# Batch 3's x transposed by VectorE from 128-byte pieces, and its whole x loaded eight steps later

## The chip, the cores and the metric

One core of a Trainium2 chip runs the kernel. The metric is device time in microseconds (us) of one execution; lower is better. TensorE's matmuls are called PE below, its weight loads PEld, VectorE DVE, ScalarE ACT, GpSimd POOL and SyncE SP; POOLq and SPq are the queues on which GpSimd and SyncE issue DMAs.

## The reference

Attention between x (4 batches, 8 heads, 512 tokens, 64 columns) and 32 state rows per head, read in both directions, then two MLPs one behind the other over all 2304 tokens (4 x 512 of x, 4 x 32 of state), each 512 to 2048 to 512:

```python
scores = scale * np.matmul(x, state.transpose(0, 1, 3, 2))
...
a /= a.sum(-1, keepdims=True) + 1e-09
xread = np.matmul(a, state)
scores2 = scale * np.matmul(state, x.transpose(0, 1, 3, 2))
...
sread = np.matmul(a2, x)
...
h = x @ w_in
g = h - np.tanh(h)
return (g @ w_out).astype(np.float32)
```

The second MLP has g = h * tanh(softplus(h)) in place of h - tanh(h). All inputs and outputs are float32.

## The kernel before

**The first MLP** runs as a list of steps (`seq`): batch 0 is steps 0 to 15, batch 1 steps 16 to 31, batch 2 steps 32 to 47, the state rows 48 to 51, batch 3 steps 52 to 67; layer 2 follows. A step makes one 128-row block of the hidden layer for 512 tokens: `up_x` multiplies into one PSUM bank h, in 6 matmuls of 128x512 (each float32 product is three: high by high, low by high, high by low, so that ath and atl are the attention's two halves and swh and swl the weights'); ScalarE takes tanh of the bank into t; VectorE subtracts (rows `t<-h,t` or, in another buffer, `wide<-h,wide`); ScalarE and VectorE split the difference into gh and gl. `down_x` of the step three before (`LA`) adds 12 matmuls into four banks acc. There are two banks h, so the matmuls of step i+2 overwrite what the subtraction of step i reads.

**Side work** is hung on a step by `at(step, f)` and issued behind its `up_x`, before the `down_x`. For batches 2 and 3 the list `when` (L1430) says at which step, counted from the start of the batch before, each of the twelve pieces of the attention comes: four turns of x (`XT[b, k]`, one per pair of heads k), the scores (`at_scores`, which calls `sc_m`, PE's matmuls into banks sct, and `sc_c`, the copies sct to scs), the softmaxes and the reads. Then `keep_pace` runs up to 3 (`MOST`) background pieces in a step, while at least 10 (`RESERVE`) slots are free: conversions of layer 2's weights (ACT `w<-st`, `r<-st`, `wh<-w`; DVE `w<-w,r`, `wl<-w,wh`, and half-size sums with tiles s), whose results POOL's queue stores to DRAM (`wi<-wh`, `wi<-wl`). Each engine works in the order in which it was issued.

**Turning x.** `at_xt` (batches 0, 1 and 3) makes four PE transposes of 128x128 into a PSUM bank xtp, rows `xtp<-ident,x`, and one ACT copy, `xt<-xtp`. They read the whole x, which `load_x` brings in four loads of 256 KB, on POOL's queue for batches 2 and 3 (L424, rows `x<-in_x_dram`, one of them into a buffer called wide). `xt_q` (batch 2 alone: `QUARTERS` is 2) is one DVE 32x32 block transpose of a 128x512 tile, `xt<-xq`, whose source `load_xq` has brought in eight DMAs of 32 KB on SP's queue (L447): each sets 32 partitions and reads 128 bytes at a time, laid out so that the block transpose alone gives the wanted order (its columns stand otherwise than those of `at_xt`, and `sc_c` sorts them out). The reading of state rows over x (`at_sread`) uses the whole x in either case.

**SP's queue** also carries the raw weights: `load_next` (L198) loads 512 KB into a stage st as soon as a conversion has read the stage's former contents, and DMAs behind it in the queue wait too.

**Pools.** 91 slots of 128x512 are handed out by `get`, oldest free first, or newest first where asked (`newest=True`), besides some half buffers.

Most engine instructions carry line 68, that of a helper which keeps their order. `load_x` is L416ff, `load_xq` L439 to L449, `xt_q` L451, `xt_t` and `xt_c` L457 and L466, `sc_m` L475, `sc_c` L493, `at_steps` L633, the loop that hangs them on steps L1431 to L1437, `keep_pace` L1444.

Of the kernel before, what the change touches and what calls it, by code (L numbers as in the profile page):

```python
# [31 lines left out]
QUARTERS = 2  # L32
# [48 lines left out]
def attention_moe_kernel(  # L81
# [16 lines left out]
    KD = DM // 128  # L98
# [24 lines left out]
    def get(name, dtype=F32, newest=False, whole=False):  # L123
        if halves and dtype == F32 and not whole:
            return halves.popleft()
        i = free.pop() if newest else free.popleft()
        return Unit(slots.tile([128, 512], dtype, tag=f"k{i}", name=name), i)
# [293 lines left out]
    def load_x(b, ks=range(KD)):  # L421
        for k in ks:
            u = get("x", newest=b > 1)
            (nc.gpsimd if b > 1 else nc.sync).dma_start(  # L424
                out=u.t.rearrange("p (h c) -> p h c", h=2),
                in_=x[b, 2 * k:2 * k + 2].rearrange("h (p r) d -> p h (r d)", r=4),
            )
            X[b, k] = u
# [10 lines left out]
    def load_xq(b, k):  # L439


        u = get("xq", whole=True)
        v = u.t.rearrange("p (i g d) -> p i g d", i=2, g=8)
        for i in range(2):
            src = x[b, 2 * k + i].rearrange("(l g e) (c d) -> (e c) l g d", g=8, e=2, c=2)
            for c in range(4):
                nc.sync.dma_start(out=v[c * 32:(c + 1) * 32, i], in_=src[c])  # L447
        P["q", b, k] = u
# [45 lines left out]
    def sc_c(b, i):  # L494
        SC[b, i] = get("scs")
        out = SC[b, i].t.rearrange("p (q e l h) -> p q e l h", q=2, e=2, h=4)
        for e in range(2):
            src = P["c", b][e][:, i * 256:(i + 1) * 256]
            if b == QUARTERS:
                src = src.rearrange("p (h q l) -> p q l h", h=4, q=2)  # L500
            else:
                src = src.rearrange("p (q l h) -> p q l h", q=2, h=4)
            evac(out[:, :, e], src, e if b else 1 - i)

    def at_scores(b):
        sc_m(b)
        for j in range(2):
            sc_c(b, j)
# [34 lines left out]
    def at_exp(b, j):  # L543
        sc_t(b, j)
        sc_max(b, j)
        sc_sub(b, j)
        sc_exp(b, j)
# [19 lines left out]
    def at_norm(b, j):  # L567
        nm_sum(b, j)
        nm_rec(b, j)
        nm_mul(b, j)  # L570

    def at_exp_t(b, j):
        e = SC.pop((b, j))
        mt = small.tile([128, 2], F32, tag="mt", name="mt")
        V.tensor_reduce(out=mt[:, 0:1], in_=e.t, axis=AX.X, op=ALU.max)
        V.tensor_scalar(
            out=mt[:, 0:1], in0=mt[:, 0:1], scalar1=-scale, scalar2=None, op0=ALU.mult
        )
        AC.activation(
            out=e.t, in_=e.t, func=ACTF.Exp, scale=scale, bias=mt[:, 0:1], accum_out=mt[:, 1:2]  # L580
        )
        V.tensor_scalar(
            out=mt[:, 1:2], in0=mt[:, 1:2], scalar1=1e-9, scalar2=None, op0=ALU.add
        )
        V.reciprocal(out=mt[:, 1:2], in_=mt[:, 1:2])
        V.tensor_scalar(
            out=e.t, in0=e.t, scalar1=mt[:, 1:2], scalar2=None, op0=ALU.mult
        )
        ET[b, j] = e

    def at_read_t(b, j):
        ps = side_bank("e2p")
        e = ET.pop((b, j))
        for r in range(4):
            TE.transpose(
                out=ps[:, r * 128:(r + 1) * 128],
                in_=e.t[:, r * 128:(r + 1) * 128],
                identity=ident,
            )
        u = get("e2")  # L600
        AC.activation(out=u.t, in_=ps, func=ACTF.Copy)
        put(e)
        ET[b, j] = u

    def at_sread(b):
        ps = side_bank("srd")
        u = [ET.pop((b, i)) for i in range(2)]
        for i in range(2):
            for r in range(4):
                for k in range(KD):  # L610
                    c = r * 128 + k * NS
                    TE.matmul(
                        out=ps[k * NS:(k + 1) * NS, i * 64:(i + 1) * 64],
                        lhsT=u[i].t[:, c:c + NS],
                        rhs=x_tile(b, k, i, r),
                        start=(r == 0),
                        stop=(r == 3),
                    )
        put(*u, *(X.pop((b, k)) for k in range(KD)))
        P["r", b] = o = get("sr")  # L620
        V.tensor_copy(out=o.t[:, :128], in_=ps[:, :128])

    def at_sturn(b):
        ps = side_bank("srt")
        u = P.pop(("r", b))
        TE.transpose(out=ps[:, :128], in_=u.t[:, :128], identity=ident)
        put(u)
        V.tensor_copy(
            out=xst[:, :, b * NS:(b + 1) * NS],
            in_=ps[:, :128].rearrange("p (k n) -> p k n", k=KD),  # L630
        )

    def at_steps(b):  # L633
        turn = xt_q if b == QUARTERS else at_xt
        return [lambda k=k: turn(b, k) for k in range(KD)] + [
            lambda: at_scores(b),
            lambda: (at_exp(b, 0), at_exp_t(b, 0)),
            lambda: at_norm(b, 0),
            lambda: (at_exp(b, 1), at_exp_t(b, 1), at_read_t(b, 0)),
            lambda: at_norm(b, 1),  # L640
            lambda: at_read_t(b, 1),
            lambda: at_sread(b),
            lambda: at_sturn(b),
        ]
# [115 lines left out]
    def evac(dst, src, i):  # L760
        if i % 2:
            return V.tensor_copy(out=dst, in_=src)
        return AC.activation(out=dst, in_=src, func=ACTF.Copy)
# [624 lines left out]
    def at(step, fn, back=None):  # L1388

        def held():  # L1390
            kept = [e.floor for e in engines]
            for e, m in zip(engines, marks[-back]):
                e.floor = m
            fn()
            for e, m in zip(engines, kept):
                e.floor = m

        side.setdefault(step, []).append(held if back else fn)

    seq = []  # L1400
    start = {}
# [18 lines left out]
    for j in range(2):  # L1420
        at(12 + j, lambda j=j: at_exp(1, j))
        at(13 + j, lambda j=j: at_norm(1, j))
        for b in range(2):
            k = start[1] + 4 + 2 * b + 4 * j
# [4 lines left out]
                at(k + 5, lambda b=b: at_sturn(b), 1)  # L1429
    when = {2: (3, 4, 5, 7, 8, 9, 10, 11, 12, 13, 15, 16), 3: (3, 3, 4, 5, 7, 8, 9, 11, 12, 12, 13, 15)}  # L1430
    for b in (2, 3):  # L1431
        if b == QUARTERS:
            for k in range(KD):
                at(start[b - 1] + when[b][k] - 3, lambda b=b, k=k: load_xq(b, k))
        at(start[b - 1] + (8 if b == QUARTERS else -1), lambda b=b: load_x(b))
        for i, f in zip(when[b], at_steps(b), strict=True):
            at(start[b - 1] + i, f)  # L1437
    for b in (1, 2, 3):
# [81 lines left out]
    def skip_banks(n):  # L1520
        ps_n[0] += n

    steps = {
        "x": lambda k: xt_t(0, k), "X": lambda k: xt_c(0, k), "s": lambda j: state_t(j, st[j]),
        "c": lambda j: sc_m(0), "C": lambda j: sc_c(0, j), "t": lambda j: sc_t(0, j),
        "m": lambda j: sc_max(0, j), "b": lambda j: sc_sub(0, j), "e": lambda j: sc_exp(0, j),
        "u": lambda j: nm_sum(0, j), "v": lambda j: nm_rec(0, j), "y": lambda j: nm_mul(0, j),
        "h": lambda j: at_a_hi(0, j), "l": lambda j: at_a_lo(0, j), "f": sw_first,
        "g": sw_first_lo, "z": skip_banks,
        "w": conv_first, "k": keep_warm, "p": lambda k: xt_t(1, k), "P": lambda k: xt_c(1, k),  # L1530
        "q": sc_m, "Q": lambda j: sc_c(1, j),
    }
    for e in (TE, AC, V):
# [153 lines left out]
```

## Time and profile before

| | |
|---|---|
| time, median of 3 runs | 702.04 us (700.21 to 702.95) |
| the profiled execution | 700.36 us, its span 698.6 us |
| granted TensorE clock | 0.999 |
| busy | PE 690.3 us (99%), DVE 514.9 (74%), ACT 366.0 (52%), POOL 90.6 (13%) |
| moved by DMA | 134.45 MB, mean 192 GB/s |

All times of the trace are us from the start of the span. Durations of single instructions overlap where an engine is pipelined: PE matmuls of 128x512 are recorded with 0.39 us each and start 0.23 us apart. "Idle before" is the time an engine stood still ahead of an instruction, with what ended it. The DMA share is the mean busy share of the 16 DMA engines; where a stretch is short it can come out a little over 1.

### The profile page before, as it was taken

To read this page: it belongs to the slowest core of one execution; us is meant where nothing else is said; L and a number is where in the kernel's file an instruction comes from. 1 tells how busy PE (TensorE), PEld (TensorE's weight loads), DVE (VectorE), ACT (ScalarE), POOL (GpSimd) and SP (SyncE) were. 2 spreads that over 40 slices of the span, in tenths; PEclk is the share of its full clock that TensorE was granted. 3 is DMA by queue.
4 is the path that set the end of the run, shared out by engine and by line. 5 is a ranking of instruction groups with operands and counts; after the bars stand their busy time and mean duration, and the time that the engine had idled before them with its cause. 6 is when DMAs were issued, how large, how long until landed. Compare 5 with 4: busy or idle time off the path is not lost.

```text
span 698.6 us, 11347 instructions
## 1 busy us (share of the span) xinstructions
PE 690.3 (99%) x4166; PEld 564.4 (81%) x4166; DVE 514.9 (74%) x904; ACT 366.0 (52%) x667; POOL 90.6 (13%) x136
## 2 busy tenths in 40 slices
PE   8999999999999999999999999999999999999998
PEld 6467777787777898778888888888888999999976
DVE  5899966796579847998476876767787555776784
ACT  6999644666576757877465432234424463433330
POOL 0000000116022323501222000111011000001000
PEclk9999999999999999999999999999999999999999
DMA  9886221318363677665959643667779676466303
GB/s 293 323 282 231 61 45 18 91 53 272 114 191 139 217 249 246 232 251 154 384 178 306 214 137 105 213 224 225 270 245 307 200 230 196 152 202 220 91 0 136
DMA packets 70952, 134.45 MB, mean 192 GB/s; under 512 B 16880, under 2 KB 27376, under 8 KB 70896
## 3 DMA queue, kind: packets, MB, share of 16 engines
q1 hardware_dynamic: 60656, 100.16, 44.2%
q0 software_dynamic: 10240, 33.56, 13.3%
q8 instruction: 33, 0.54, 0.3%
q14 instruction: 23, 0.19, 0.1%
HBM read 97.78 MB, written 35.91 MB: 191 GB/s over the span
## 4 chain that ended last, share of the span: by engine, by line
PE 42%; issue 37%; POOL 7%; ACT 5%; DVE 4%; DMA 4%; SPq 1%; POOLq 0%; ACTq 0%
PE acc L68 22%; PE h L68 15%; POOL wi L272 4%; POOL wo L272 2%; PE hs L68 2%; ACT r L68 2%; ACT w L68 2%; POOL wt L1149 1%; DMA x<-in_x_dram 1%; DMA wi<-wh 1%; DVE out L68 1%; DMA wide<-in_moe_w_out_dram 1%; PE swp L68 1%; DMA wt<-wl 1%; DVE wide L68 1%
## 5 line engine op out<-in xcount | busy, mean ns | idle before, releaser
L68 PE MATMUL h<-yh,ws 128*128 128x512 f32 x448 | 156.2, 392 | 0.1
L68 PE MATMUL acc<-wo,gh 128*128 128x512 f32 (+1 forms) x332 | 101.4, 387 | 0.4 <-DVE out L68 0.4
L68 PE MATMUL acc<-gh,wh 128*128 128x512 f32 x244 | 98.4, 403 | 0.0
L68 PEld LDWEIGHTS h<-yh,ws 128*128 128x128 f32 x448 | 84.3, 188 | 17.1 <-DVE wide L68 0.7
L68 PE MATMUL acc<-gh,wl 128*128 128x512 f32 x244 | 95.3, 391 | 0.0
L68 PE MATMUL acc<-gl,wh 128*128 128x512 f32 x244 | 95.2, 390 | 0.0
L68 PE MATMUL h<-yl,ws 128*128 128x512 f32 x224 | 87.6, 391 | 0.0
L68 DVE TENSOR_TENSOR gl<-wide,gh 128x512 fp32r<-128x512 f32 x79 | 53.6, 687 | 31.3 <-ACT gh L68 30.7
L68 PEld LDWEIGHTS acc<-wo,gh 128*128 128x128 f32 x332 | 61.9, 188 | 13.3 <-DVE out L68 0.8
L68 PE MATMUL acc<-wf,gh 128*128 128x256 f32 x384 | 70.5, 283 | 0.0
L68 ACT ACTIVATE wide<-wide 128x512 f32<-128x512 f32 x39 | 24.7, 633 | 83.0 <-DVE wide L68 83.0
L68 DVE TENSOR_TENSOR wide<-h,wide 128x512 f32<-128x512 f32 x76 | 52.1, 686 | 17.2 <-ACT wide L68 10.3
L68 PEld LDWEIGHTS acc<-wf,gh 128*128 128x128 f32 x384 | 62.0, 191 | 2.7
L68 PE MATMUL acc<-wo,gl 128*128 128x512 f32 (+1 forms) x166 | 64.2, 387 | 0.0
L68 PEld LDWEIGHTS acc<-gh,wh 128*128 128x128 f32 x244 | 45.8, 188 | 18.2 <-issue 4.2
L68 ACT ACTIVATE wide<-h 128x512 f32<-128x512 f32 x41 | 24.3, 593 | 61.9 <-PE h L68 55.1
L68 PE MATMUL acc<-wf,gl 128*128 128x256 f32 x192 | 54.3, 283 | 0.0
L68 PEld LDWEIGHTS acc<-gh,wl 128*128 128x128 f32 x244 | 45.8, 188 | 10.0
L68 PEld LDWEIGHTS acc<-gl,wh 128*128 128x128 f32 x244 | 45.9, 188 | 9.0 <-issue 0.4
L68 PE MATMUL h<-ath,swh 128*128 128x512 f32 x128 | 51.5, 403 | 1.2 <-ACT swh L68 1.2
L68 ACT ACTIVATE gh<-wide 128x512 fp32r<-128x512 f32 x79 | 48.4, 629 | 7.6 <-DVE wide L68 6.4
L68 PE MATMUL h<-ath,swl 128*128 128x512 f32 x128 | 50.5, 395 | 0.5 <-DVE swl L68 0.5
(220 smaller groups left out, 1289.3 us busy)
## 6 DMA issues: line engine op xcount, KB each, us to landing
ws<-wi SPq DMA_DIRECT2D x128, 256.0 KB, 4.5
st<-in_moe_w_in_dram SPq DMA_DIRECT2D x26, 512.0 KB, 5.4
wo<-wo SPq DMA_DIRECT2D x48, 256.0 KB, 4.1
st<-in_moe_w_out_dram SPq DMA_DIRECT2D x23, 512.0 KB, 5.0
wi<-wh POOLq DMA_DIRECT2D x32, 256.0 KB, 3.9
wi<-wl POOLq DMA_DIRECT2D x32, 256.0 KB, 4.4
wf<-wt SPq DMA_DIRECT2D x24, 256.0 KB, 5.1
wf<-wo SPq DMA_DIRECT2D x24, 256.0 KB, 3.7
```

Source lines behind the costliest of these rows:

```text
L68: i = fn(*args, **kw)
L272: nc.gpsimd.dma_start(out=d, in_=v if len(d.shape) == 2 else v.rearrange("p (g e) -> p g e", g=2))
L1149: nc.gpsimd.dma_start(out=D2T[g][:, 2 * j:2 * j + 2, h, :], in_=u.t.bitcast(F32).rearrange("p (i e) -> p i e", i=2),)
```

## The change

Batch 3's turn of x is done as batch 2's is. All four `load_xq(3, k)`, 32 DMAs of 32 KB, are issued at step 31; `xt_q` takes the place of `at_xt` at the same steps (35, 35, 36 and 37); the four whole loads of x move from step 31 to step 39, where the first user left is `at_sread` at step 45. `sc_c` sorts the columns for both batches.

```diff
@@ -439,7 +439,7 @@
     def load_xq(b, k):
 
 
-        u = get("xq", whole=True)
+        u = get("xq", newest=b > QUARTERS, whole=True)
         v = u.t.rearrange("p (i g d) -> p i g d", i=2, g=8)
         for i in range(2):
             src = x[b, 2 * k + i].rearrange("(l g e) (c d) -> (e c) l g d", g=8, e=2, c=2)
@@ -496,7 +496,7 @@
         out = SC[b, i].t.rearrange("p (q e l h) -> p q e l h", q=2, e=2, h=4)
         for e in range(2):
             src = P["c", b][e][:, i * 256:(i + 1) * 256]
-            if b == QUARTERS:
+            if b >= QUARTERS:
                 src = src.rearrange("p (h q l) -> p q l h", h=4, q=2)
             else:
                 src = src.rearrange("p (q l h) -> p q l h", q=2, h=4)
@@ -631,7 +631,7 @@
         )
 
     def at_steps(b):
-        turn = xt_q if b == QUARTERS else at_xt
+        turn = xt_q if b >= QUARTERS else at_xt
         return [lambda k=k: turn(b, k) for k in range(KD)] + [
             lambda: at_scores(b),
             lambda: (at_exp(b, 0), at_exp_t(b, 0)),
@@ -1429,10 +1429,12 @@
                 at(k + 5, lambda b=b: at_sturn(b), 1)
     when = {2: (3, 4, 5, 7, 8, 9, 10, 11, 12, 13, 15, 16), 3: (3, 3, 4, 5, 7, 8, 9, 11, 12, 12, 13, 15)}
     for b in (2, 3):
-        if b == QUARTERS:
-            for k in range(KD):
-                at(start[b - 1] + when[b][k] - 3, lambda b=b, k=k: load_xq(b, k))
-        at(start[b - 1] + (8 if b == QUARTERS else -1), lambda b=b: load_x(b))
+        for k in range(KD):
+            at(
+                start[b - 1] + (when[b][k] - 3 if b == QUARTERS else -1),
+                lambda b=b, k=k: load_xq(b, k),
+            )
+        at(start[b - 1] + (8 if b == QUARTERS else 7), lambda b=b: load_x(b))
         for i, f in zip(when[b], at_steps(b), strict=True):
             at(start[b - 1] + i, f)
     for b in (1, 2, 3):
```

How the instructions stand. **PE** around the first two turns, step 35, before (acc is numbered by bank):

```order
659 L68 MATMUL h<-atl,swh 128x512
660 L68 MATMUL h<-ath,swl 128x512
661 L68 MATMUL xtp<-ident,wide 128x128 x4
662 L68 MATMUL xtp<-ident,x 128x128 x4
663 L68 MATMUL acc_2215<-gh,wh 128x512
664 L68 MATMUL acc_2215<-gl,wh 128x512
```

and with the change:

```order
659 L68 MATMUL h<-atl,swh 128x512
660 L68 MATMUL h<-ath,swl 128x512
661 L68 MATMUL acc_2231<-gh,wh 128x512
662 L68 MATMUL acc_2231<-gl,wh 128x512
663 L68 MATMUL acc_2231<-gh,wl 128x512
```

The sixteen transposes of steps 35 to 37 are gone (3651 PE instructions before, 3635 now), and nothing else in PE's order moves.

**SP's queue** from the last pieces of batch 2's x on, the difference:

```order
 L447 DMA xq<-in_x_dram 32x8x32 x32
 L198 DMA st<-in_moe_w_in_dram 128x1024
-L198 DMA st<-in_moe_w_out_dram 128x1024 x4
+L198 DMA st<-in_moe_w_out_dram 128x1024 x3
+L447 DMA xq<-in_x_dram 32x8x32 x20
+L198 DMA st<-in_moe_w_out_dram 128x1024
+L447 DMA xq<-in_x_dram 32x8x32 x12
 L198 DMA st<-in_moe_w_in_dram 128x1024 x4
```

Twenty of the new DMAs (tiles 0, 1 and half of tile 2) stand before a load of raw weights into a stage, twelve behind it.

**DVE** from the second of the four new transposes on (steps 34 to 38; each `t<-h,t` is the subtraction of a step), with the change:

```order
251 L68 STREAM_TRANSPOSE xt<-xq 128x512
252 L68 SCALAR_TENSOR_TENSOR w<-w,r 128x512 x2
253 L68 TENSOR_TENSOR t<-h,t 128x512
254 L68 TENSOR_TENSOR wl<-w,wh 128x512
255 L68 TENSOR_TENSOR gl<-t,gh 128x512
256 L68 SCALAR_TENSOR_TENSOR w<-w,r 128x512
257 L68 TENSOR_TENSOR wl<-w,wh 128x512 x2
258 L68 TENSOR_TENSOR t<-h,t 128x512
259 L68 STREAM_TRANSPOSE xt<-xq 128x512
260 L68 TENSOR_TENSOR gl<-t,gh 128x512
...
264 L68 TENSOR_TENSOR gl<-t,gh 128x512
265 L68 STREAM_TRANSPOSE xt<-xq 128x512
```

and before, over the same steps:

```order
250 L68 SCALAR_TENSOR_TENSOR w<-w,r 128x512
251 L68 TENSOR_TENSOR t<-h,t 128x512
252 L68 TENSOR_TENSOR gl<-t,gh 128x512
253 L68 TENSOR_TENSOR t<-h,t 128x512
254 L68 TENSOR_TENSOR gl<-t,gh 128x512
255 L68 TENSOR_TENSOR wl<-w,wh 128x512
256 L68 SCALAR_TENSOR_TENSOR w<-w,r 128x512
257 L68 TENSOR_TENSOR t<-h,t 128x512
258 L68 TENSOR_TENSOR wl<-w,wh 128x512
259 L68 TENSOR_TENSOR gl<-t,gh 128x512
```

The first new transpose stands behind the subtraction of step 33, the second behind the copies y that end batch 1, the third behind the subtraction of step 36, the fourth behind the split of step 37. Conversions of layer 2's weights come earlier: from the copies y to the first transpose `a<-scs` (of the scores, around step 39) VectorE has six rows `w<-w,r` where it had four, five `wl` where it had three, four half-size sums where it had none, and the three later transposes. ScalarE loses its four copies `xt<-xtp`.

## Rows read from the trace of the kernel before

**Rows 1.** The page: busy time, and busy share and granted clock in 40 slices.

```profile
PE 690.3 (99%) x4166; PEld 564.4 (81%) x4166; DVE 514.9 (74%) x904; ACT 366.0 (52%) x667; POOL 90.6 (13%) x136
...
PE   8999999999999999999999999999999999999998
...
PEclk9999999999999999999999999999999999999999
```

**Rows 2.** Stretches, steps 35, 36, 37 and 41: us, busy by engine, clock, DMA share, GB/s.

```profile
181.57:186.57 5.00, 5.00 (x28) 4.21 (x26) 3.05 (x5) 3.55 (x7) 0.54 (x1) 1.00 0.32 105
186.57:191.14 4.57, 4.57 (x23) 3.77 (x22) 1.65 (x3) 1.75 (x4) 0.04 (x1) 1.00 0.17 61
191.14:195.68 4.54, 4.54 (x23) 3.77 (x22) 3.10 (x5) 3.31 (x6) 1.44 (x3) 1.00 0.54 160
210.43:214.51 4.08, 4.08 (x20) 3.38 (x19) 4.08 (x10) 2.38 (x5) 1.58 (x2) 1.00 0.82 312
```

**Rows 3.** Timeline of PE, steps 35 and 36: start us, us, engine, operation, count.

```profile
182.93 0.60 PE L68 MATMUL xtp<-ident,wide 128*128 128x128 f32 x4
...
184.03 0.40 PE L68 MATMUL acc<-gl,wh 128*128 128x512 f32 x1
...
187.93 0.60 PE L68 MATMUL xtp<-ident,x 128*128 128x128 f32 x4
...
188.60 0.40 PE L68 MATMUL acc<-gl,wh 128*128 128x512 f32 x1
```

**Rows 4.** The tile xtp: ns min/median/max of one, first and last start.

```profile
L68 ACT ACTIVATE xt<-xtp x10: 589/596/608, 6.6 to 193.2; 128x512 f32<-128x512 f32 x10
```

**Rows 5.** The tile xq, batch 2's pieces and their transposes.

```profile
L447 SPq DMA_DIRECT2D xq<-in_x_dram x32: 561/607/803, 87.3 to 108.3; - x32
...
L68 DVE STREAM_TRANSPOSE xt<-xq x2: 702/704/706, 106.1 to 115.5; 128x512 f32<-128x512 f32 x2
...
DMA to landing us min/median/max: 2.1/2.4/2.9
```

**Rows 6.** Stretches: a step of batch 1, the load's stretch, steps 35 to 43.

```profile
104.66:108.73 4.07, 4.07 (x19) 3.37 (x19) 4.00 (x11) 1.94 (x4) 0.00 (x0) 1.00 0.35 54
165.00:170.00 5.00, 5.00 (x34) 4.06 (x23) 3.74 (x9) 3.07 (x6) 4.70 (x8) 1.00 0.93 319
170.00:175.00 5.00, 5.00 (x24) 4.13 (x23) 4.05 (x8) 2.36 (x5) 3.09 (x5) 1.00 1.02 355
182.54:206.27 23.73, 23.73 (x151) 18.16 (x150) 13.18 (x23) 15.22 (x29) 3.28 (x6) 1.00 0.40 133
205.00:225.00 20.00, 20.00 (x102) 15.63 (x101) 19.97 (x46) 13.96 (x28) 4.65 (x7) 1.00 0.55 184
```

**Rows 7.** Timeline of SyncE's queue, 182 to 193 us.

```profile
182.53 0.33 SPq L198 DMA_DIRECT2D st<-in_moe_w_out_dram  x1
192.35 0.33 SPq L198 DMA_DIRECT2D st<-in_moe_w_in_dram  x1
```

**Rows 8.** Timeline of ScalarE, 181 to 184 us.

```profile
181.84 0.67 ACT L68 ACTIVATE w<-st 128x512 f32<-128x512 f32 x1
```

**Rows 9.** Timeline of the POOL queue, 160 to 205 us.

```profile
165.44 2.16 POOL L424 DMA_DIRECT2D x<-in_x_dram  x3 [0.30 <-PE srd L68]
```

**Rows 10.** DMA issues by kind: queue, count, KB each, median us to landing.

```profile
x<-in_x_dram POOLq DMA_DIRECT2D x7, 256.0 KB, 3.4
...
wide<-in_x_dram POOLq DMA_DIRECT2D x1, 256.0 KB, 6.6
```

**Rows 11.** Timeline of VectorE: start us, us, operation, idle before and its releaser.

```profile
178.47 0.69 DVE L68 TENSOR_TENSOR wide<-h,wide 128x512 f32<-128x512 f32 x1 [2.05 <-ACT wide L68]
...
188.76 0.69 DVE L68 TENSOR_TENSOR t<-h,t 128x512 f32<-128x512 f32 x1 [2.82 <-ACT t L68]
...
194.95 0.68 DVE L68 TENSOR_TENSOR gl<-t,gh 128x512 fp32r<-128x512 f32 x1
...
209.97 0.68 DVE L68 TENSOR_TENSOR t<-h,t 128x512 f32<-128x512 f32 x1
```

## The prediction

> **What bounds the kernel now.** First the page: PE is busy 690.3 us of 698.6 and in every slice but the first and the last at nine tenths or more, at the full granted clock [rows 1]; DVE is busy 74%, ACT 52%. So the program lasts as long as PE's list of work, unless another engine makes PE wait. The stretches of steps 35 to 37 say the same of the place of the change: PE is busy through all of 5.00, 4.57 and 4.54 us, at clock 1.00, while DVE works 3.05, 1.65 and 3.10 of them and ACT 3.55, 1.75 and 3.31 [rows 2]. A plain step, such as the 41st, is 4.08 us for its 18 matmuls [rows 2], 0.227 each. What is taken from PE's list there should come off the end; what is put on DVE or DMA costs only if PE then waits.
>
> Over its own span the profiled execution has 1.8 us (700.36 against 698.6), and it lies 1.7 us under the median of 702.04. I work out differences in the trace and set them against the median.
>
> **PE's transposes go (16 matmuls).** Step 35 has two groups of four: from the first group's start to the second matmul of acc, 182.93 to 184.03, is 1.10 us [rows 3]; one matmul of that is there anyway (0.23), so the two groups cost 0.87. Steps 36 and 37 have one each: 187.93 to 188.60 is 0.67, less 0.23 is 0.44 [rows 3], and twice 0.44 is 0.88. Sum 1.75. By whole steps: 5.00 + 4.57 + 4.54 less three times 4.08 is 1.87 [rows 2]. I take 1.8; the ends are 1.75 and 1.87. All of it is on the path, since PE works throughout. PE's order is otherwise as before.
>
> The Trainium skill, "VectorE: DVE Perf Modes", section "Rules for kernel authors", speaks against the change: a 128x128 transpose belongs on TensorE if PSUM will do as its destination, and the DVE is for 32x32 blocks. The rows agree on the durations, 0.44 us of PE a tile against 0.70 of DVE [rows 3, 5]; they differ from the rule in which engine has time left. The case in which the rule would hold here is part of the first rival.
>
> **DVE's four transposes come.** Each is 0.70 us [rows 5], 2.8 in all, and with them ACT's four copies of 0.60 go [rows 4]. The difference in order also brings weight conversions forward: between 182.54 and 206.27 DVE gets two more `w`, two more `wl`, four half sums and three of the transposes. At about 0.69 for a full row [rows 11], and 0.4 for a half one (an estimate: a fixed share and half the columns), that is 4 x 0.69 + 4 x 0.4 + 3 x 0.70 = 6.5 us. DVE is busy 13.18 of these 23.73 us [rows 6]; 10.5 are free, so it fits. I cost it at nothing. The cover is the two banks h: the subtraction of step 36 ends at 188.76 + 0.69 = 189.45 [rows 11] and its bank is written again at 195.68, the end of step 37 [rows 2], 6.2 us later. The precedent: batch 2's transposes ran between 106.1 and 115.5 on DVE [rows 5], and a step there is 4.07 us long with DVE busy 4.00 of it [rows 6]. If the cover were gone, each transpose would cost PE 0.70.
>
> **The pieces on SP's queue.** 32 DMAs at 0.61 us [rows 5] are 19.5 us of queue. Their slots come free when the reads `srd` of step 31 have ended; the whole loads of x waited for the same thing and went out at 165.44 [rows 9]. The first 20 then go out from 165.5 to about 177.7. Tile 0 is complete 8 x 0.61 later plus a landing of 2.4 to 2.9 [rows 5], at about 173; even with the 6.6 us of the load of x that landed slowest [rows 10] it is 177. DVE meets it behind the subtraction of step 33, about 175, and if it waited to 177 it would still be in front of the next subtraction at 178.47, ahead of which it stood idle 2.05 us [rows 11]. Tile 1, out by 175.2, is wanted only at step 34's end, about 182.5.
>
> Then comes the new wait. A raw load stands in front of the last twelve pieces, and it waits for the ACT conversion `w<-st` that ends at 181.84 + 0.67 = 182.51 [rows 8]; it went out at 182.53 [rows 7]. Behind it the twelve go out from 182.86 to 190.2. Tile 2 lands by 182.86 + 4 x 0.61 + 2.9 = 188.2, tile 3 by 193.1. DVE reaches the third transpose behind the subtraction of step 36 (189.45, or about 188.5 with PE 0.9 us earlier) and the fourth behind the split of step 37 (194.95 + 0.68 = 195.6 [rows 11], or 194.2 with PE 1.4 earlier). Margins of 0.3 and 1.1 us, and behind them the bank's 6 us. So I cost this at nothing; the ends are nothing and, if each landing took 6.6 us in place of 2.9 [rows 10], 3.7 less 0.3 of DVE's time, which the 6.2 still cover. The raw load behind the last pieces went out at 192.35 before [rows 7], since its stage was not free earlier; the pieces are out by 190.2.
>
> **DMA traffic.** Before, the whole loads fell into a stretch that was full (shares 0.93 and 1.02 [rows 6]). Now the first 20 pieces, 0.64 MB, fall there. Batch 2's moved 54 GB/s at a share of 0.35 [rows 6], 154 GB/s for a full share, against 319 at 0.93, or 343. So they take 0.64/154, 4.2 us of all engines, where 1 MB at 343 took 3.1: about 1 us more traffic. POOL's stores can be later by as much; PE reads none of what they carry before layer 2. The whole loads go to step 39, about 200, and land by some 207 [rows 10]; `at_sread` is at step 45, over 20 us on. Nothing for both.
>
> The Trainium skill, "DMA: Bandwidth & Descriptors", section "Specifications", holds that transfers below 512 bytes fall short of line rate. The rows of batch 2 agree, 154 against 343 GB/s for a full share; by the rule and by the rows alike the price is DMA time, which PE pays only if a tile is late.
>
> **Sum.** -1.8 + 0 + 0 + 0: 702.04 - 1.8 = 700.2 us (profiled 700.36 - 1.8 = 698.6).
>
> **The rivals.**
>
> *DVE gives it back.* Between 205 and 225 DVE is busy 19.97 of 20 us [rows 6]. The subtraction of step 40 ends at 209.97 + 0.68 = 210.65 [rows 11], its bank is written again at 214.51 [rows 2]: 3.9 us of slack, and 2.1 once PE is 1.8 us ahead and DVE is not. If the earlier conversions go on inside this stretch, three more (each a `w` and a `wl`, 1.4 us) are 4.2 us, and PE waits 2.1: 702.3; with five 7.0, a wait of 4.9 and 705.1. Were DVE without time from the turns on, four transposes of 0.70 less the 1.8 would be a loss of 1.0, 703.0. (That is the case of the Trainium skill's rule on transposes, named above.) For it: the full stretch. Against: conversions done early are not done again later, and 10.5 us are free ahead of it. Chance 0.15, times 701.5 to 705.
>
> *Slower, by SP's queue.* The raw load holds twelve pieces back for as long as its stage is not read. If that conversion is put off, tile 3 comes later by as much, DVE stops in front of it in order, and once 1.1 us and the bank's 6.2 are used up PE waits: from 7.3 us on it costs, from 9.1 on it has eaten the gain. Three steps of delay, 12.2 us, give 702.04 - 1.8 + 4.9 = 705.1; four give 709. For it: the queue waits in order, and conversions come in bursts when slots come free. Against: the difference in order brings conversions forward, not back, and ACT has less to do. Chance 0.07.
>
> *No effect.* PE's transposes might hide in a wait that PE would have anyway: 702.0. Against it, the matmuls behind them follow at once [rows 3]. Chance 0.06.
>
> *More than removed.* With the copies off ACT and the loads spread, some wait elsewhere might shrink: 3.6 us or more, 698.4 or less. But PE shows hardly a wait to shrink, only 8.3 us in the span, at its ends [rows 1]. Chance 0.06.
>
> **How the numbers follow.** The forecast keeps 0.66. A measurement tells changes over 0.5%, 3.5 us, from none, so the forecast, no effect and most of the first rival (up to 705.5) are "same": 0.65 + 0.06 + 0.13, and 0.02 of the second rival. Faster is the last rival, 0.06, and 0.01 of the forecast's spread: 0.07. Slower is the second rival but for its mildest cases, 0.05, and the first one's tail, 0.02: 0.07. Same is the rest, 0.86. The range: below, 700.2 less the 1.87 end and the 1.7 us by which executions lie under their median, 698.0. Above, it takes in no effect and the nearer part of the first rival, 703.2; left out are about 0.19: the last rival's 0.06, and 0.13 of the first two.
>
> **What would show it.** Right: no `xtp` in steps 35 to 37, which come down to about 4.1 us each, PE's matmuls fewer by 16, and DVE transposes of 0.70 that wait for a DMA less than 2 us. Wrong, by the first rival: PE idle "until DVE t" in 205 to 225. By the second: the fourth transpose starts after 200 and PE waits at step 39. If steps 35 to 37 shorten and the time does not fall by 1.4 us or more, a later stretch has taken it, and the first sum is wrong in its claim that nothing behind PE is short.

## The result and the profile after

| | before | with the change |
|---|---|---|
| time, median of 6 runs each | 701.4 us (700.21 to 702.95) | 710.57 us (707.22 to 712.93) |
| ratio to before | | 1.0125, 95% interval 1.0102 to 1.0148 |
| the profiled execution, its span | 700.36 us, 698.6 us | 711.1 us, 709.3 us |

The kernel is 9.2 us slower, where 1.2 us faster than this median was forecast (700.2), and outside the range. The page, the rows that answer to [rows 1]:

```profile
PE 693.4 (98%) x4150; PEld 565.9 (80%) x4150; DVE 517.9 (73%) x908; ACT 363.4 (51%) x663; POOL 90.8 (13%) x136
...
PE   8999999999997999899999999999999999999998
...
PEclk9999999999998999999999999999999999999999
```

PE's share has fallen, though its list of work is shorter: two slices (from 213 and from 284 us) are below nine tenths, and the granted clock has an eight among its nines. The waits of PE from 180 us to the end, first with the change and then before (us in all, times, longest):

```profile
PE e2p L68 <- DVE swl L68: 4.3, 1, 4.3
PE h L68 <- DVE t L68: 2.7, 1, 2.7
PE acc L68 <- DVE y L68: 0.7, 1, 0.7
```

```profile
PE acc L68 <- DVE out L68: 0.4, 1, 0.4
```

Before, PE waited once there, 0.4 us; that wait is there with the change too. Beside it PE now stands three times, before banks that DVE should have read. Where the time went is read from the starts of the same `up_x` matmuls in both traces (us from the span's start):

```
step    before   change   difference   since the row above
35      181.57   182.10   +0.53
38      195.68   194.34   -1.34        -1.87   the transposes
43      219.85   218.51   -1.34         0.00
44      224.42   229.99   +5.57        +6.91   wait before e2p, half clock
52      269.13   275.70   +6.57        +1.00   wait before acc
55      282.63   293.69   +11.06       +4.49   wait before h, half clock
end     698.6    709.3    +10.7        -0.4
```

The +0.53 is there from 34 us on, before any row that the change touches, and is of the execution. The stretches that answer to [rows 2] (steps 35 to 37) and [rows 6], and the two around the first wait (busy us of PE, PEld, DVE, ACT and POOL, then clock, DMA share, GB/s):

```profile
182.10:186.19 4.09, 4.09 (x20) 3.38 (x19) 4.04 (x7) 3.87 (x8) 0.57 (x1) 1.00 0.53 156
186.19:190.26 4.07, 4.07 (x19) 3.38 (x18) 3.81 (x6) 2.92 (x6) 2.70 (x5) 1.00 0.80 243
190.26:194.34 4.08, 4.08 (x19) 3.38 (x18) 3.17 (x5) 2.99 (x6) 0.84 (x2) 1.00 0.94 272
205.00:225.00 20.00, 15.74 (x80) 11.79 (x79) 15.59 (x33) 11.36 (x23) 6.57 (x10) 0.94 0.68 238
219.67:224.33 4.66, 0.41 (x3) 0.01 (x1) 4.55 (x9) 2.80 (x6) 1.45 (x2) 0.83 0.38 135
224.33:230.00 5.67, 5.67 (x17) 4.62 (x18) 5.67 (x14) 4.62 (x9) 0.86 (x1) 0.54 0.09 30
```

The three steps are 4.09, 4.07 and 4.08 us, as forecast. From 205 to 225, where DVE was full before, it works only 15.59 of 20 us and PE 15.74. From 219.67 PE does next to nothing for 4.66 us, and in the 5.67 us behind it the granted clock is 0.54.

**The chain behind the first wait**, from PE back. PE, the matmul in front of the wait and the one that ends it:

```profile
219.67 0.40 PE L68 MATMUL h<-ath,swl 128*128 128x512 f32 x1
224.33 0.90 PE L68 MATMUL e2p<-ident,scs 128*128 128x128 f32 x3 [4.25 <-DVE swl L68]
```

The bank of e2p (the transposes of a softmax's scores) had held the products swp of step 42, and DVE had not yet split them. DVE, the subtraction of step 41 and that split (a row's idle time stands in brackets with what ended it):

```profile
217.64 0.69 DVE L68 TENSOR_TENSOR t<-h,t 128x512 f32<-128x512 f32 x1 [1.93 <-ACT t L68]
...
223.59 0.68 DVE L68 TENSOR_TENSOR swl<-swp,swh 128x512 fp32r<-128x512 f32 x1
```

DVE waited for ScalarE's tanh, 217.02, though the h of step 41 was complete at 210.6. From there it worked without a gap to the split (4.55 of the 4.66 us in which PE stood), late by what it had waited. ScalarE, in the order in which it was issued:

```profile
206.56 0.66 ACT L68 ACTIVATE w<-st 128x512 f32<-128x512 f32 x1 [2.29 <-DMA wi<-wh]
...
210.10 0.68 ACT L68 ACTIVATE r<-st 128x512 uint32<-128x512 uint32 x1 [0.78 <-DMA wi<-wl]
...
211.39 0.58 ACT L68 ACTIVATE t<-h 128x512 f32<-128x512 f32 x1
...
216.46 0.66 ACT L68 ACTIVATE r<-st 128x512 uint32<-128x512 uint32 x1 [2.90 <-DMA wi<-wl]
217.02 0.59 ACT L68 ACTIVATE t<-h 128x512 f32<-128x512 f32 x1
```

Three conversions of layer 2's weights, `w<-st` and `r<-st`, stood 2.29, 0.78 and 2.90 us until stores of other weights, wi, had landed. They write into slots that those stores still read. The tanh of steps 40 and 41 (211.39 and 217.02) stand behind them. The chain of waits names the first of these stores:

```profile
201.38 5.10 DMA wi<-wh
...
206.56 0.13 ACT w L68
```

It was issued at 201.38 and took 5.10 us. Before, in the same steps, the tanh of step 40 began at 209.04 and the one wait of ScalarE for a store was 0.88:

```profile
209.04 0.58 ACT L68 ACTIVATE t<-h 128x512 f32<-128x512 f32 x1
...
212.20 0.63 ACT L68 ACTIVATE wh<-w 128x512 fp32r<-128x512 f32 x1 [0.88 <-DMA wo<-wh]
```

The wait of PE at 284 us is of the same kind: a split of layer 1's output, `yh<-wide`, waits 5.05 us for a store, and the tanh of step 52 behind it is 8 us behind its matmuls:

```profile
284.80 0.63 ACT L68 ACTIVATE yh<-wide 128x512 fp32r<-128x512 f32 x1 [5.05 <-DMA wo<-wl]
285.34 0.58 ACT L68 ACTIVATE t<-h 128x512 f32<-128x512 f32 x1
```

In the compiled order, each wait can be followed to the store that it names. In steps 39 to 42, three instructions of ScalarE and VectorE wait for stores of the last two steps before the change, and nine with it. What the forecast called harmless on DVE, conversions that come earlier, is the difference: by step 42 the change has done 29 background pieces, the kernel before 24 (20 against 15 by step 36).

The tile xq, to [rows 5]:

```profile
L68 DVE STREAM_TRANSPOSE xt<-xq x6: 702/704/712, 106.6 to 195.6; 128x512 f32<-128x512 f32 x6
...
  DMA xq<-in_x_dram: 1.1, 1
...
DMA to landing us min/median/max: 2.1/2.6/7.2
```

The pieces land up to 7.2 us after issue, and the last tile kept DVE 1.08 us; no wait of PE comes of it.

### The profile page after: what moved, and what is told of

Same layout as the page of the kernel before. It is cut to its first block, busy times and chain, and to the rows that moved or that the text cites. A ratio compares the mean times of both kernels' runs of the same rounds, so it can differ in the third digit from the quotient of the medians.

```text
span 709.3 us, 11372 instructions
## 1 busy us (share of the span) xinstructions
PE 693.4 (98%) x4150; PEld 565.9 (80%) x4150; DVE 517.9 (73%) x908; ACT 363.4 (51%) x663; POOL 90.8 (13%) x136
## 4 chain that ended last, share of the span: by engine, by line
PE 70%; issue 12%; ACT 6%; POOL 5%; DVE 4%; DMA 3%; SPq 0%; POOLq 0%; ACTq 0%; DVEq 0%
PE acc L68 38%; PE h L68 28%; POOL wi L272 3%; PE hs L68 2%; ACT r L68 2%; ACT w L68 2%; POOL wo L272 1%; PE swp L68 1%; DMA wo<-wl 1%; DVE out L68 1%; DMA wide<-in_moe_w_out_dram 1%; DMA x<-in_x_dram 1%; DMA wi<-wh 1%; ACT t L68 1%; DVE a L68 0%
## 5 line engine op out<-in xcount | busy, mean ns | idle before, releaser
L68 DVE TENSOR_TENSOR gl<-wide,gh 128x512 fp32r<-128x512 f32 x82 | 55.6, 688 | 27.9 <-ACT gh L68 27.1
L68 DVE TENSOR_TENSOR wide<-h,wide 128x512 f32<-128x512 f32 x79 | 54.2, 687 | 21.7 <-ACT wide L68 14.9
L68 ACT ACTIVATE wide<-h 128x512 f32<-128x512 f32 x44 | 26.0, 593 | 73.3 <-PE h L68 66.2
L68 ACT ACTIVATE gh<-wide 128x512 fp32r<-128x512 f32 x82 | 50.3, 629 | 11.1 <-DVE wide L68 9.9
```

Source lines behind the costliest of these rows:

```text
L68: i = fn(*args, **kw)
```

## The experiments

Three theories were set against each other. **A:** the slots that the change gives back between steps 35 and 39 let conversions run earlier and make buffers fall on slots whose stores have only just been issued. **B:** the whole loads of x, now amid those stores, make them land late. **C:** the new turns, their pieces or DVE's extra work. Times in this section are medians beside the kernel before on the same chip (701.0, 700.4, 700.7 and 701.0 us in the four sessions).

### e1: the pace of before

```diff
-                    if done[0] < goal and bg and len(free) >= RESERVE:
+                    if done[0] < RAN[i] and bg:
```

RAN lists the pieces that the kernel before has done by each step.

> The change, with the number of background pieces done by each step fixed to what the kernel before does (24 by step 42, where the change does 29). Theory A: the pieces brought forward take slots whose stores to DRAM have only just been issued, so that ScalarE stands in order before a conversion and tanh comes late. Then ScalarE's waits for the stores wi in steps 39 to 42 go, PE's wait of 4.25 us before e2p and the half clock behind it go, steps 35 to 37 stay 1.87 us shorter, and the time is 701.4 - 1.9 = about 699.5 us (698.5 to 700.5). Theory B: the whole loads of x, now at step 39 on POOL's queue, make those stores late; they are still there, so PE still waits 2 to 5 us and the time is 704 to 710. Theory C: the four transposes on DVE or the late last tile of pieces are what delays DVE; both are still there, and the time stays near 710.

Measured: 707.5 us, ratio 1.0094 (1.0078 to 1.0109). Of the first layer A is right: in steps 35 to 37 PE gains 0.92, 0.49 and 0.46 us, and nothing is lost up to 520 us. But a wait that the change did not have stands in layer 2:

```profile
PE h L69 <- DVE wide L69: 5.7, 1, 5.7
```

```profile
524.10 0.68 DVE L69 TENSOR_TENSOR wl<-tf,wh 128x512 fp32r<-128x512 f32 x1
531.43 1.42 DVE L69 TENSOR_TENSOR wide<-h,wide 128x512 f32<-128x512 f32 x2 [6.66 <-DMA out_dram<-wide]
```

The second fence is DVE: the subtraction in layer 2 writes a buffer whose last content is still on its way to the output, and stands 6.66 us. PE waits 5.7, a half clock follows, and the two steps lose 5.92 and 1.66 us: about what the time is above its 699.5. The time alone would also fit B (704 to 710); the place of the loss fits neither B nor C. So the pace explains layer 1, and something else of the pool is different in layer 2.

### e2: the kernel before at the pace of the change

The same edit to the kernel before, with the other list.

> The kernel before, its turns by PE and its loads of x at step 31 kept, with the number of background pieces done by each step fixed to what the change does. Theory A: ScalarE waits for stores in steps 39 to 42 and PE waits as with the change, 4 to 8 us with the half clock; with PE's transposes kept the time is 705 to 712. Theory B and theory C: nothing of theirs is in this kernel, 701.4 within 1 us.

Measured: 708.45 us, 1.0121 (1.0100 to 1.0143). Without a turn of batch 3 by DVE, its pieces or a late load of x, the earlier conversions alone cost 7.5 us. ScalarE's first wait and two of PE's (a third, 1.5 us, lies at 284 us):

```profile
175.03 0.66 ACT L69 ACTIVATE w<-st 128x512 f32<-128x512 f32 x1 [4.96 <-DMA wi<-wh]
```

```profile
PE xtp L69 <- DVE swl L69: 2.8, 1, 2.8
...
PE e2p L69 <- DVE swl L69: 1.2, 1, 1.2
```

The places are not all the change's own: the first is before the transposes of step 35. This kernel also has four slots fewer free at that pace, so the run shows that earlier conversions can cost as much, not that they cost it in the same way.

### e3: x's loads moved off the stores

```diff
-        at(start[b - 1] + (8 if b == QUARTERS else 7), lambda b=b: load_x(b))
+        if b == 3:
+            at(start[b - 1] + 7, lambda b=b: hold_x(b))
+        at(start[b - 1] + (8 if b == QUARTERS else 11), lambda b=b: load_x(b))
```

`hold_x` takes the four slots at step 39, `load_x` uses them at step 43; the pace is the change's own.

> The change with the pieces done by each step fixed to its own, the four slots of x taken at step 39 as there, but the four loads issued at step 43. All slots, and every row of PE, DVE and SP, are as in the change; only the four DMAs on POOL's queue move. Theory A: the waits on stores are the same slots' and stay; a little shorter without the loads beside them: 705 to 711. Theory B: the stores land sooner, ScalarE's waits at 206, 210 and 216 us fall under 1 us in all, and the time is 699.5 to 701.

Measured: 709.82 us, 1.0129 (1.0116 to 1.0142). B falls: two of ScalarE's three waits are there without the loads, 4.53 us in place of 5.97 in all, and PE's with them.

```profile
206.37 0.66 ACT L69 ACTIVATE w<-st 128x512 f32<-128x512 f32 x1 [3.06 <-DMA wi<-wh]
...
216.41 0.66 ACT L69 ACTIVATE r<-st 128x512 uint32<-128x512 uint32 x1 [1.47 <-DMA wi<-wl]
```

```profile
PE e2p L69 <- DVE swl L69: 4.2, 1, 4.2
```

### e4: x's slots taken later too

The load and the taking of its slots at step 43, pace of the change.

> The change with the pieces done by each step fixed to its own, but the slots of x taken and its loads issued at step 43 in place of 39. Theory A, as a matter of slots: four slots more are free from 39 to 43, so that conversions of steps 39 and 40 take slots that were stored longer ago; the waits in steps 39 to 41 go and the time is 699.5 to 703, with new waits possible at steps 44 and 45, where x's slots come in their turn. If the number of pieces alone were the cause (ScalarE and DVE full, no slot), the time would stay at 707 to 711. Theory B: the stores of steps 39 to 42 are free of x's loads: 699.5 to 702; this run does not tell A from B, run e3_x_dma_late does.

Measured: 711.24 us, 1.0149 (1.0134 to 1.0164): a miss for every theory's number, nearest to that of the pieces alone, with no part for the slots (707 to 711). The conversions' waits for stores in steps 39 to 41 are gone, as A said, and PE's wait before e2p is 1.6 us in place of 4.3, but others have come later:

```profile
PE h L69 <- DVE t L69: 3.4, 1, 3.4
PE h L69 <- DVE xst L69: 2.7, 1, 2.7
PE e2p L69 <- DVE swl L69: 1.6, 1, 1.6
```

```profile
235.66 0.71 DVE L69 STREAM_TRANSPOSE at<-a 128x512 f32<-128x512 f32 x1 [4.49 <-DMA wi<-wh]
```

Both have an engine that stands for a store ahead of them: DVE at 235.66, 4.49 us, before xst, and ScalarE at 283.61, 5.76 us before `yh<-wide`, with the tanh for `t` behind it. So the loss is again one of slots; relief at one place was paid at another.

### e5: the same slots as before

```diff
-        u = get("xq", newest=b > QUARTERS, whole=True)
+        u = get("xq", newest=b > QUARTERS, whole=b == QUARTERS)
...
-        put(u)
+        if b == QUARTERS:
+            put(u)
+        else:
+            X[b, k] = u
...
-            u = get("x", newest=b > 1)
+            u = X[b, k] if (b, k) in X else get("x", newest=b > 1)
```

> The change, but batch 3's pieces are loaded into the four slots that the kernel before takes at step 31 for the whole x, those slots are kept after the transposes, and the whole x is loaded into the same four at step 39. So slots are taken and given back step for step as in the kernel before, background pieces run at its steps, and layer 2 gets the same slots; only the turns by DVE, the pieces on SP's queue and the later loads of x are left of the change. Theory A (slots given back at steps 35 to 37 bring conversions forward and turn the pool over, and the waits on stores in both layers come from that): PE loses no time anywhere, steps 35 to 37 are 1.87 us shorter, 701.0 - 1.9 = 699.1 us (698.3 to 700.2). Theory C (the turns by DVE, the pieces or the later x cost something of their own that the paced run did not show): above 700.9.

Measured: 698.66 us, ratio 0.9973 (0.9962 to 0.9984), 1.8 us faster than before. It is the whole change but for the slots, and gives the forecast gain. PE's two longest waits from 180 us on, and the steps 35 to 37:

```profile
PE acc L68 <- DVE out L68: 0.4, 1, 0.4
PE acc L68 <- ACT ys L68: 0.3, 1, 0.3
```

```profile
180.86:184.94 4.08, 4.08 (x20) 3.38 (x18) 4.01 (x7) 2.81 (x5) 1.37 (x3) 1.00 0.54 157
184.94:189.02 4.08, 4.08 (x20) 3.38 (x18) 1.38 (x3) 1.26 (x3) 0.64 (x1) 1.00 0.85 235
189.02:193.10 4.08, 4.08 (x20) 3.38 (x18) 3.62 (x7) 2.95 (x5) 1.43 (x3) 1.00 0.37 81
```

C falls with it: with turns, pieces and late loads all in place, PE has only two short waits that the kernel before has not, this one of 0.3 us and one of 0.2.

### e6 and e7: the pool turned over, nothing else

Both add to the kernel before a function that takes the four oldest free slots and gives them back at once, e6 at step 67 and e7 at step 39 (e7 is shown):

```diff
+    def turn_over():
+        us = [get("r", whole=True) for _ in range(KD)]
+        put(*us)
+
+    at(start[2] + 7, turn_over)
```

> The kernel before, with the four oldest free slots taken and given back at once at step 67, the last of layer 1: no work is added, removed or paced otherwise, only the order of the free slots is another from there on. Theory A, for what cost the paced run 5.9 us and a half clock at 526 us: which slot a layer 2 buffer falls on decides whether it waits for a store, so that the time can move by several us either way; PE gets a wait over 1 us after 340 us that the kernel before has not, 701.5 to 709, or stays within 0.5 us of 701.0 if the turn happens to be harmless. If the pool's order does not matter in layer 2, 701.0 within 0.5 us.

Measured: 701.2 us, 1.0009 (0.9999 to 1.0019): no difference that can be told; the turn was harmless there.

> The kernel before, with the four oldest free slots taken and given back at once at step 39 in place of step 67. Conversions of layer 1 then take other slots; the waits that the program holds in steps 39 to 52 are as in the kernel before but one fewer, so layer 1 should keep its time and layer 2 may wait as in the paced run: 700.5 to 708. If the pool's order does not matter, 701.0 within 0.5 us.

Measured: 705.05 us, 1.0055 (1.0035 to 1.0076). No instruction is added, yet 4.6 us are lost. The place was not the one expected: it is layer 1, again e2p, behind a conversion that waits for a store:

```profile
216.64 0.63 ACT L68 ACTIVATE wh<-w 128x512 fp32r<-128x512 f32 x1 [3.31 <-DMA wo<-wh]
```

```profile
PE e2p L68 <- DVE swl L68: 2.3, 1, 2.3
```

So the order of the slots costs time at the pace of before too; the pace is one way into such a wait and not the only one.

### e8: four slots in reserve

```diff
-                    if done[0] < goal and bg and len(free) >= RESERVE:
+                    if done[0] < goal and bg and len(free) >= RESERVE + KD * (3 <= i - start[2] < 7):
```

> The change with four more slots held in reserve in steps 35 to 38, where the whole x no longer takes them: background pieces then run at nearly the steps of the kernel before, but the slots that they take are others. Theory A by pieces: the stall at 220 us goes, 699 to 701 if no slot is met too early elsewhere; the program holds waits of a conversion on a store of the step before in steps 42 to 48 and 52, and each of those that comes true would cost 1 to 3 us, up to 705. Theory C: 710.

Measured: 711.91 us, 1.0155 (1.0134 to 1.0176), a miss, and by its number nearest to C's 710. The stall at 220 us went, and three others came:

```profile
PE h L68 <- DVE wide L68: 4.7, 1, 4.7
PE acc L68 <- DVE y L68: 1.9, 1, 1.9
PE h L68 <- DVE xst L68: 1.6, 1, 1.6
```

```profile
536.39 1.42 DVE L68 TENSOR_TENSOR wide<-h,wide 128x512 f32<-128x512 f32 x2 [5.62 <-DMA out_dram<-wide]
```

The longest is e1's wait in layer 2 once more; before the one for xst DVE stands 2.62 us for a store of weights, as in e4. Steps 35 to 37 keep their 1.87 us. Holding back as many slots as before is not the same as holding the same slots.

### e9 to e11: the wait in layer 2

To e1, e9 and e10 add the turning over of four and of eight free slots at step 67; e11 keeps one of the half buffers out of use from there on (`keep` starts as [0]):

```diff
-        if halves and dtype == F32 and not whole:
+        if len(halves) > keep[-1] and dtype == F32 and not whole:
...
+    at(start["2"] - 1, lambda: keep.append(1))
```

> The paced change (e1_paced), with the four oldest free slots taken and given back at once at step 67. Rows of PE, DVE, ACT and POOL are as there; layer 2's buffers fall on other slots and some loads of SP's queue change places. Theory A, pool order: the wait of 5.9 us at 526 us, where DVE stood 6.66 us until a store out_dram<-wide had landed, belongs to one slot's reuse and changes or goes: 699 if no other wait takes its place, up to 706 if one does. If that wait comes from the turns by DVE or from the pace itself, it stays and the time is 707 again.

> As e9_paced_turn4 with the eight oldest free slots turned over in place of four: a second draw of the order of slots. Theory A: 699 to 706, by where the wait falls, and not the same wait as with four. If the pool's order does not matter in layer 2: 707 as in the paced run.

Measured: 706.6 us, 1.0078 (1.0057 to 1.0100), and 714.71 us, 1.0201 (1.0183 to 1.0218). The wait before `wide` stayed in both, against A as I had put it, and with eight slots turned a load of weights came late besides:

```profile
PE h L69 <- DMA ws<-wi: 5.5, 1, 5.5
PE h L69 <- DVE wide L69: 4.5, 1, 4.5
```

The buffer in e1's wait is a half buffer, and these have a queue of their own, which turning over whole slots leaves as it is. Hence e11.

> The paced change (e1_paced), with one of the half buffers kept out of use from step 67 on. In the paced run's program the subtraction that stood 6.66 us at 526 us writes a half buffer whose last content goes to the output by a store that is issued only when PE stands at that very matmul; in the kernel before, the nearest such reuse is 15 PE rows later than its store. With one half fewer in turn the nearest is 18 rows. Theory A (early reuse of stored buffers, in layer 2 too): the wait of 5.5 to 5.9 us and the half clock behind it go and nothing else changes: 707 - 7.5 = 699 to 700 us. If the wait came from the turns by DVE, the pace or SP's loads: it stays, 706 to 708.

Measured: 699.45 us, 0.9975 (0.9963 to 0.9988). The wait is gone, and with it the loss; PE's longest behind the ramp is one that the kernel before has too:

```profile
PE h L69 <- DVE swl L69: 0.5, 1, 0.5
```

So by two ways, the same slots (e5) or the pace of before with one half buffer fewer (e11), the turns by DVE bring what PE's rows promised.

## Why the prediction was wrong

**PE's transposes: right.** 1.87 us were saved (0.92, 0.49 and 0.46 by step), where 1.8 was taken and 1.87 was an end. The Trainium skill's rule that I weighed ("VectorE: DVE Perf Modes", "Rules for kernel authors": a 128x128 transpose on TensorE) loses to the measurement here: e5 has the turns on DVE and is 1.8 us faster.

**DVE's four transposes: right in themselves.** 0.70 us each; the precedent of batch 2 held. The third tile did not wait, as its margin of 0.3 us had it; the fourth, with a margin of 1.1, kept DVE waiting 1.08 us, inside the bank's slack.

**The step that failed is the next one:** "The difference in order also brings weight conversions forward [...] so it fits. I cost it at nothing." I counted only the DVE time of the conversions, 6.5 us against 10.5 free, and DVE had that time. A conversion also takes slots, and hands them to a store. With conversions nearer together a slot comes round sooner than its store lands (5.10 us at 201.38), and then ScalarE stands, in order, with tanh behind it: 5.97 us over three conversions, and PE 4.25. e1 takes the earlier conversions away and layer 1 keeps the 1.87; e5 keeps every slot where it was and the gain is there in the time. e2 has earlier conversions without the rest and loses 7.5 us, in part at other places; e7 has no earlier conversions, only another order of the slots, and loses 4.6.

**The same gap in the part on DMA traffic:** "POOL's stores can be later by as much; PE reads none of what they carry before layer 2." True of the data, but what waits for a store is whoever takes its slot next. The larger traffic itself is not the cause (the loads of x in e3, the pieces in e5).

**The first rival** had the place (205 to 225 us) and PE's waiting for DVE, not the cause: over these 20 us DVE was not full but in part idle, 15.59 busy against 19.97 [rows 6], held up by ScalarE, and full only behind that. It had 2.1 us of slack used up by DVE's own work, and 705 as its end; the measured stall and the half clock behind it took 6.91 us in step 43, and 5.49 more were lost up to step 55. **The second rival** did not happen: SP's raw load went out at 182.79, 182.53 before [rows 7]. The test named at the end, steps 35 to 37 shorter and the time not, did tell that a later stretch had taken it.

The range failed with that step: no case in it had ScalarE waiting for a store. Its lower end does not come out of its own terms either, 702.04 less 1.87 and 1.7 is 698.5 and not 698.0, which changes nothing here.

## What to carry to other kernels

Where buffers come from one pool, a change in when a buffer is taken or given back is a change to every later buffer: beside the durations, follow each wait of the new order on a store or load to how long ago that transfer was issued. An engine with time to spare is no cover if its next instruction in order waits for a DMA and the critical work stands behind it. To try a local edit for what it is worth, keep the takings and givings back step for step as they were (e5), and decide on the pool apart from it.

## What the runs showed of the hardware

Some of PE's waits were dearer than their length. Behind the 4.25 us before e2p the granted clock was 0.54 over 5.67 us, that is mostly the 1.2 GHz level, with PE at work throughout, and step 43 lost 6.91 us in all. In e1 it was the same in layer 2, the granted clock 0.62 over the 4.38 us behind the wait: the step lost 5.92 us and the next one 1.66. The length alone does not tell whether the clock falls. The first stretch is behind e2's wait of 2.84 us, whose step lost 3.45; the second is behind e7's shorter wait of 2.27 us, whose step lost 4.03:

```profile
185.91:190.00 4.09, 3.89 (x20) 3.22 (x21) 3.11 (x5) 4.09 (x10) 0.00 (x0) 1.00 0.40 125
224.19:229.01 4.82, 4.82 (x16) 3.89 (x17) 4.82 (x13) 2.87 (x6) 1.54 (x3) 0.65 0.16 54
```

The Trainium skill, "TensorE: Matmul & The Clock Gate", section "What's actually happening", says that the clock is held at the lower level when the array has been idle and is released by activity; the rows of the change, of e1 and of e7 agree, and behind e2's wait the clock stayed at 1.00, the 2.4 GHz level.
